# The overflow rows spread in two passes, batches 0 to 3 first and 4 to 7 added, and a new written order

## The chip, the cores and the metric

The kernel runs on one core of a Trainium2 chip. The metric is the device time of one execution, in microseconds (us). TensorE does the matmuls (PE in the profile), VectorE (DVE) and ScalarE (ACT) do the elementwise work and empty the matmul results out of PSUM, GpSimd (POOL) issues nearly all transfers, and the sync engine (SP) issues the first few.

## The reference

Linear attention and, on its result, a layer of eight experts with hash routing. Attention, for 8 batches of 8 heads, 576 tokens and head width 64, then the experts over all 4608 tokens of width 512:

```python
q_s = softmax(q, axis=-1); k_s = softmax(k, axis=2)
kv  = np.einsum('bhsd,bhse->bhde', k_s, v)
x   = np.einsum('bhsd,bhde->bhse', q_s, kv)      # then tokens x 512
expert_idx = token_ids * 2654435761 % 8
for e in range(8):
    mask = expert_idx == e
    h = np.maximum(x[mask] @ w1[e], 0.0)         # 512 -> 1024
    out[mask] = h @ w2[e]                        # 1024 -> 512
```

## The kernel before

Every expert has 640 slots for tokens: 72 for each of the 8 batches (576, five blocks of rows with the last half full) and 64 more for its overflow, the tokens that did not fit into the 72 of their batch. An index stage of about 11 us computes from the token ids which row of q goes into which slot. Then the rows of q are gathered slot by slot with indirect transfers, softened, transposed, and multiplied by their batch's `kv`, so that the expert's input stands in slot order, transposed, in `XT`. The overflow tokens of all experts are gathered apart, by batch pair, multiplied by `kv` (`xov0` to `xov3`, one for two batches each), and then spread to the experts' overflow slots (`XTov`) with one-hot matrices `Qs`.

The work is cut into named steps. A list written out by hand, `ORDER`, says in which order they are issued; each engine carries out its own in that order, and so does GpSimd with its transfers. A set `SWAP` says which of the copies that may go to either of ScalarE and VectorE leave their usual engine. The steps, with e an expert, b a batch, i a block or a part:

- `K b`, `V b`, `G e_i`, `GO_i`, `W e1_i`, `W e2_i`: transfers, on GpSimd's queue (K0 to K2 on the sync engine's): k and v of a batch, gathers of q rows for an expert's block or the overflow, and the halves of an expert's two weight matrices. L781, L785, L395, L508.
- `EK b`, `MK b`, `EQ e_i`: on ScalarE, the exponentials of k (two instructions, L354 and L355), the column of ones beside v, the exponential of a gathered block (L406).
- `KV b`: on TensorE, 20 matmuls to k-transposed times v (L372); `SC b`: on VectorE, four instructions that divide by the sums into `kvrs` (L381 to L387).
- `SM e`, `ML e` (with a or b for the blocks): on VectorE, the row sums of the exponentials and their reciprocals (L418 to L420), and the scaling (L424). `TP e_i`, `TC e_i`: transposes on TensorE (L436), copy out of PSUM (L879, L875 for the overflow `TCO`).
- `PP e_lo r`, `PC e_lo r`: matmuls of transposed q with `kvrs` (L447, L459), batches from lo, quarter r of the width; copy into `XT` (L907, L913).
- `XP n`, `XC n`: the same for the overflow of batches 2n and 2n+1 (L469, L886). `SH r`, `SD r`: the spreading of quarter r, four matmuls that add up over n (L476), and its copy into `XTov` (L482).
- `FND`, `FDD`, `QS`, `ROP`, `ROD`: the overflow's index work.
- `A e_lo_i`, `R e_lo_i`: the first expert product from slot lo on (L523) and its relu. `A0_576_0` is the one that reads `XTov` for expert 0; for the others `OV e` copies `XTov` into `XT`. `B e_blk`, `C e_blk`, `S e_blk`: the second product of a block (L545), its copy out (L936, L938) and its scatter into the output (L550).

`NAME*n` in the list puts n warming matmuls ahead of that step's own (L345). PSUM has eight banks in three kinds, and a step of TensorE waits until a bank of its kind has been emptied: two of T (XP, SH, B and others), two of Q (TP and PP of the first four experts), two double ones of S (KV, A, later PP). The second buffer of the weights holds the exponentials of k until the last KV is done, so the second expert's weights wait for that. Odd batches' k has one buffer, even batches' two; a load waits for the exponential that reads its buffer, and v waits for the KV of the batch whose buffer it takes.

Of the kernel before, what the change touches and what calls it, by code (L numbers as in the profile page):

```python
# [701 lines left out]
W31_0 EQ5_3 PP2_32 G5_0 PP2_01 PC2_01 G6_0 EQ5_2 R1_320_0 B1_1 EQ4_0 PC2_32 PP2_33 R1_320_3 PP2_30 PC2_33
EQ5_4 PC2_30 W31_1 G5_1 B1_0 C1_1 C1_0 PP2_02 SM4a PP2_03 B1_2 PC2_02 PP2_31 PC2_03 OV5 OV4 PP2_00 EQ4_3 B1_3
C1_2 W22_0 G7_0 PC2_31 PC2_00 A2_0_0 PP2_63 W22_1 G7_4 ML4a PP2_60 G6_3 A2_0_1 PC2_63 PP2_61 R2_0_0 EQ5_0
R2_0_1 PC2_61 PC2_60 S0_1 B1_4 OV2 A2_320_1 R2_320_1 EQ5_1 SM5b A3_0_1 W32_1 R3_0_1 S0_3 G7_3 A2_0_2 G6_4
TP4_0 S1_1 S0_0 R2_0_2 A2_320_3 R2_320_3 A2_320_2 ML5b A2_0_3 SM5a ML5a W32_0 C1_4 R2_320_2 A3_320_2 R2_0_3
A3_0_0 R3_320_2 G6_1 R3_0_0 A2_320_0 A3_0_3 TP5_3 TC4_0 TC5_3 R2_320_0 TP4_2 B2_3 R3_0_3 C1_3 A3_0_2 A3_320_0
EQ4_4 W41_0 R3_0_2 R3_320_0 TP5_0 TC5_0 A3_320_3 A3_320_1 C2_3 W41_1 B2_1 SM4b ML4b TP5_2 R3_320_3 R3_320_1
C2_1 EQ7_1 B2_4 EQ6_1 PP4_01 TC4_2 PP4_00 TC5_2 G7_2 EQ7_0 C2_4 TP4_3 EQ7_3 PC4_01 B3_1 PC4_00 S1_2 W51_1 S2_4
TC4_3 C3_1 PP4_30 EQ6_0 EQ6_2 S1_0 B2_0 PP4_60 EQ6_4 PC4_30 OV6 PC4_60 PP4_31 B2_2 SM6a C2_0 PP4_61 W51_0 ML6a  # L710
PC4_31 C2_2 EQ7_2 PC4_61 OV7 EQ7_4 A4_0_1 SM7b S1_4 B3_4 C3_4 R4_0_1 TP6_2 A4_320_0 B3_3 R4_320_0 W42_0
A4_320_2 R4_320_2 S3_4 SM7a EQ6_3 A4_0_3 TP6_0 TC6_2 R4_0_3 S2_1 W42_1 A4_320_1 TC6_0 R4_320_1 A4_320_3
R4_320_3 B3_2 ML7b ML7a A5_320_2 A5_320_1 R5_320_2 C3_2 A4_0_2 TP7_3 S2_2 S3_1 R4_0_2 R5_320_1 TP7_0 B3_0
A5_0_0 TC7_0 C3_3 R5_0_0 SM6b TP7_2 A4_0_0 W52_1 TC7_2 R4_0_0 A5_0_2 C3_0 S1_3 B4_1 R5_0_2 A5_320_3 R5_320_3
PP6_00 B4_0 A5_0_1 PC6_00 ML6b A5_320_0 C4_1 C4_0 TP6_3 R5_0_1 PP6_01 B4_3 TC7_3 W52_0 S3_0 R5_320_0 B4_4 C4_4
# [295 lines left out]
```

## Time and profile before

| | us |
|---|---|
| Median of 3 runs | 224.19 (224.01 to 224.94) |
| Profiled execution | 224.46 |
| Its span, first to last instruction | 222.6 |
| TensorE busy in it | 189.1 (85%) |
| VectorE, ScalarE, GpSimd busy | 137.8, 116.6, 122.9 |

The span is what the trace shows; the time of the execution is longer by what lies around it. In timelines a row is one or more like instructions of one engine, with the idle time ahead of it and what ended it in brackets; lengths of successive rows of TensorE overlap a little, since matmuls are pipelined, so costs are best taken from one start to the next. The granted clock is the share of TensorE's full clock.

### The profile page before, as it was taken

The page shows a single profiled execution, that of the slowest core. Times are in us where ns is not written, and L with a number is a line of the kernel's source. Part 1 is how long each engine was busy: PE and PEld are TensorE (multiplying, and loading weights), DVE is VectorE, ACT ScalarE, POOL GpSimd, SP SyncE. Part 2 cuts the span into 40 slices and gives each one's busy share as a digit, 9 for nine tenths or more (in the row PEclk, how much of TensorE's full clock was granted, in tenths as well). Part 3 has the DMA queues.
Part 4 walks back from the last instruction along what each step waited for, and adds up shares of the span by engine and source line. Part 5 has one row for each costly group of instructions (what it writes and reads, how often), then busy time and mean ns, then how long its engine had stood idle before and what let it go on. Part 6 is the DMA issues. An engine that isn't in the chain of part 4 may idle for free.

```text
span 222.6 us, 3981 instructions
## 1 busy us (share of the span) xinstructions
PE 189.1 (85%) x1533; PEld 124.1 (56%) x1533; DVE 137.8 (62%) x259; ACT 116.6 (52%) x189; POOL 122.9 (55%) x160
## 2 busy tenths in 40 slices
...
GB/s 209 321 329 389 234 345 329 322 245 296 292 280 274 292 247 267 221 244 233 266 308 216 239 146 155 148 165 3 175 234 167 188 186 195 284 110 135 166 165 85
DMA packets 13543, 50.67 MB, mean 228 GB/s; under 512 B 2650, under 2 KB 2650, under 8 KB 12496
## 3 DMA queue, kind: packets, MB, share of 16 engines
...
q1 hardware_dynamic: 576, 3.71, 4.3%
...
## 4 chain that ended last, share of the span: by engine, by line
issue 38%; POOL 21%; PE 20%; DMA 11%; DVE 6%; ACT 2%; POOLq 1%; DVEq 0%
POOL out_dram L550 12%; PE ph L523 7%; DMA kraw<-in_k_dram 4%; PE po L545 4%; DMA out_dram<-ob,sidx 3%; DMA w1r<-in_moe_w_dram 3%; POOL raw L395 3%; PE t L372 2%; POOL w1r L508 2%; PE t L436 2%; PE t L476 2%; POOL w2r L508 2%; DVE A L126 1%; PE t L447 1%; PE t L469 1%
## 5 line engine op out<-in xcount | busy, mean ns | idle before, releaser
L545 PE MATMUL po<-w2r,hT 128*128 128x512 f16 (+2 forms) x328 | 74.8, 374 | 0.0
L523 PE MATMUL ph<-XT,w1r 128*128 128x320 f16 (+2 forms) x512 | 74.6, 297 | 0.0
L536 ACT ACTIVATE hT<-ph 128x640 f16<-128x640 f32 (+3 forms) x58 | 40.5, 703 | 55.3 <-PE ph L523 54.6
L550 POOL DMA_INDIRECT out_dram<-ob,sidx x40 | 42.6, 1065 | 44.7 <-DVE ob L938 29.6
L523 PEld LDWEIGHTS <-w1r 128*128 128x128 f16 x544 | 49.3, 98 | 21.2
L395 POOL DMA_INDIRECT raw<-in_q_dram,gidx x40 | 42.9, 1071 | 20.7 <-issue 4.9
L938 DVE TENSOR_SCALAR ob<-po 128x512 f32<-128x512 f32 x34 | 23.1, 683 | 43.8 <-PE po L545 39.4
L545 PEld LDWEIGHTS <-hT 128*128 128x128 f16 x328 | 30.9, 98 | 30.4
L418 DVE TENSOR_REDUCE rq<-qs 128x16 f32<-128x1024 f16 (+1 forms) x18 | 26.1, 1450 | 3.8 <-ACT qs L406 3.7
L424 DVE TENSOR_TENSOR qs<-qs,rq 128x1024 f16<-128x1024 f16 (+1 forms) x18 | 26.1, 1456 | 0.4
L406 ACT ACTIVATE qs<-raw 128x512 f16<-128x512 f32 (+1 forms) x40 | 23.6, 625 | 0.8 <-DMA raw<-in_q_dram,gidx 0.8
L436 PE MATMUL t<-ident,qs 128*128 128x128 f16 (+1 forms) x176 | 15.8, 226 | 4.8 <-ACT qT L879 2.6
L879 DVE COPY qT<-t 128x512 f16<-128x512 f16 (+3 forms) x18 | 8.5, 478 | 15.6 <-PE t L436 15.3
L508 POOL DMA_DIRECT2D w2r<-in_moe_w_dram x16 | 9.5, 595 | 14.3 <-PE po L545 10.1
L436 PEld LDWEIGHTS <-qs 128*128 128x128 f16 (+1 forms) x176 | 12.0, 103 | 9.1 <-issue 4.3
L372 PE MATMUL t<-v,w1r 128*128 128x129 f16 x64 | 8.0, 293 | 7.5 <-ACT v L360 7.5
L508 POOL DMA_DIRECT2D w1r<-in_moe_w_dram x16 | 9.5, 595 | 5.8 <-PE ph L523 3.7
L372 PEld LDWEIGHTS <-w1r 128*128 128x128 f16 x64 | 6.9, 139 | 7.5 <-issue 7.4
L372 PE MATMUL t<-v,w2r 128*128 128x129 f16 x64 | 5.9, 243 | 5.9 <-DVE rec L381 5.9
L907 DVE CAST XT<-t 128x288 f16<-128x288 f32 (+2 forms) x18 | 7.9, 453 | 4.2 <-PE t L447 3.9
L913 ACT CAST XT<-px 128x864 f16<-128x864 f32 (+1 forms) x7 | 5.6, 811 | 8.6 <-PE px L459 8.6
L879 ACT COPY qT<-t 128x512 f16<-128x512 f16 (+2 forms) x14 | 7.9, 581 | 3.9 <-PE t L436 3.9
...
## 6 DMA issues: line engine op xcount, KB each, us to landing
...
```

The lines of the kernel that those rows point to most:

```text
L372: nc.tensor.matmul(pkv[:, r // 2, r % 2, 0:129], lhsT=k16t[:, f] if last else k16[:, c, f], rhs=v16s[e][:, c * NPAIR + r, 0:129] if last e ...
L395: nc.gpsimd.indirect_dma_start(out=raw[0:w, :], out_offset=None, in_=self.q[:, :], in_offset=bass.IndirectOffsetOnAxis(ap=idx[0:w, i:i + 1 ...
L406: self.nc.scalar.activation(q16[0:w, i].rearrange("p h d -> p (h d)"), raws[i][0:w, :], ACT.Exp)
L418: nc.vector.reduce_sum(rv, qv, axis=AX.X)
L424: nc.vector.tensor_tensor(out=qf, in0=qf, in1=rv.rearrange("p i h -> p (i h)").unsqueeze(2) .to_broadcast([w, (hi - lo) * H_, DH_]), op=AL ...
L436: nc.tensor.transpose(pv[:, r, o:o + w[j]], q16[0:w[j], j, 2 * r:2 * r + 2, :] .rearrange("p h d -> p (h d)"), self.ident[0:w[j], 0:w[j]])
L508: self.nc.gpsimd.dma_start(w[what - 1][:, 2048 * i:2048 * i + 2048], src[e, :, 2048 * i:2048 * i + 2048])
L523: nc.tensor.matmul(p, lhsT=w1r[:, dc, f[i] * 128:(f[i] + 1) * 128], rhs=X[:, dc, :], start=(dc == 0), stop=(dc == DC - 1))
L536: self.nc.scalar.activation(to, fro, ACT.Relu)
L545: nc.tensor.matmul(po[:, 0:d.stop - d.start], lhsT=hT[:, fc, blk * 128:(blk + 1) * 128], rhs=w2r[:, fc, d], start=(fc == 0), stop=(fc == F ...
L550: sc = self.nc.gpsimd.indirect_dma_start(out=self.out[:, :], out_offset=bass.IndirectOffsetOnAxis(ap=self.ix.sidx[:, e, blk:blk + 1], axis=0),
L938: nc.vector.tensor_scalar(out=obs[e, blk][:, d], in0=po[e, blk, x][:, 0:d.stop - d.start], scalar1=1.0 / SX, scalar2=None, op0=ALU.mult)
```

## The change

`shared` takes the batch pairs that it adds up. `SH r` now spreads pairs 0 and 1 (batches 0 to 3), `SD r` copies that into `XTov`; a new step `SI r` spreads pairs 2 and 3, and a new step `SE r` adds its result to what stands in `XTov`, on VectorE. All of `ORDER` and `SWAP` is written anew. In the new list the steps ahead of the first expert product and a few behind it, and the last ones, are these (the middle is left out; it holds the same steps as before in another order):

```diff
@@ -470,16 +470,21 @@
                                  rhs=self.kvrs[2 * n + j][:, r, :], start=(j == 0), stop=(j == 1))
         return pt
 
-    def shared(self, xovs, Qs, r):
+    def shared(self, xovs, Qs, r, ns):
         pr = self.bank("T")
-        for n in range(NBP):
+        for n in ns:
             self.nc.tensor.matmul(pr[:], lhsT=xovs[n][:, r * 128:(r + 1) * 128], rhs=Qs[n],
-                                  start=(n == 0), stop=(n == NBP - 1))
+                                  start=(n == ns[0]), stop=(n == ns[-1]))
         return pr
 
     def spread(self, pr, r):
         put = self.nc.scalar.copy if other(f"SD{r}", r % 2 == 1) else self.nc.vector.tensor_copy
         put(self.XTov[:, :, r, :], pr[:].rearrange("p (e i) -> p e i", e=E_MOE))
+
+    def join(self, pr, r):
+
+        x = self.XTov[:, :, r, :]
+        self.nc.vector.tensor_tensor(out=x, in0=pr[:].rearrange("p (e i) -> p e i", e=E_MOE), in1=x, op=ALU.add)
 
 
 def other(name, put):
@@ -678,48 +683,48 @@
 
 SWAP = set("""
-TC0_4 PC0_00 PC0_43 R0_0_3 TCO_3 R0_0_2 R0_0_1 PC0_62 PC0_60 PC0_63 SD2 SD1 TC1_1 SD0 PC1_40 C0_1 PC1_00
-PC1_01 C0_2 TC2_3 C0_0 PC1_43 TC3_3 TC2_2 TC2_1 TC3_0 R1_0_1 PC2_32 R1_320_3 C1_1 C1_0 PC4_01 PC4_00 PC4_31
-TC6_3 C7_4a C7_4b
+TCO_1 PC1_03 SD0 PC0_01 TCO_2 PC0_42 PC1_01 PC0_41 XC2 PC0_62 R0_0_2 PC0_61 R0_432_1 C0_4 TC3_3 TC3_4 TC2_0
+PC2_60 R1_0_2 R1_0_0 PC2_01 PC2_30 PC2_03 PC2_33 C0_3 R2_320_1 C1_1 R3_320_2 R3_320_0 C2_2 PC4_31 C2_1 C2_0
+PC6_01 C6_4 R7_0_1 C7_4a C7_4b
 """.split())
 
 ORDER = """
-MK0 EK1 MK1 CNT G0_2 EK0 G0_0 EQ0_2 OVA ZO1 KV1 G0_1 EQ0_0 KV0 EQ0_1 ZO0 OHA FND K3 FDD G0_3 V2 EK2 QS SM0a
-EQ0_3 G0_4 MK2 EQ0_4 EK3 V3 SC0 GO_1 SC1 KV2 ML0a SM0b K4 TP0_0 G1_4 MK3 TP0_1 KV3 GO_0 EQO_0 V5 ML0b K5 EQO_1
-GO_3 TC0_0 TC0_1 SMOa TP0_3 MLOa TC0_3 SC3 TP0_4 GO_2 TC0_4 SC2 ROP V4 MK5 TP0_2 TC0_2 TPO_1 K6 EK5 EQO_3 V6
-ROD TPO_0 TCO_0 TCO_1 MK4 XP1 EQO_2 PP0_03*4 SMOb EK4 MLOb EK6 G1_3 KV5 W01_0 SC5 PP0_00 MK6 PC0_00 EQ1_4 KV4
-SC4 PC0_03 PP0_40*4 EQ1_3 W01_1 PP0_41 XP0 XC1 PC0_41 PP0_43 K7 PC0_43 PC0_40 TPO_2 PP0_01 SM1b TCO_2 PC0_01
-V7 KV6 PP0_02 PP0_42 PC0_42 PC0_02 XP2 G1_2 XC0 TPO_3 EK7 MK7 ML1b A0_0_3 G3_4 SC6 G1_0 A0_0_2 R0_0_3 TCO_3
-TP1_4 G2_1 G1_1 R0_0_2 EQ1_2 TC1_4 A0_0_1 W02_1 TP1_3 KV7 R0_0_1 TC1_3 A0_0_0 SC7 XP3 PP0_62 PP0_60 XC2 G2_4
-EQ1_0 PC0_62 G3_3 PC0_60 PP0_63 EQ1_1 PP0_61 G2_3 XC3 PC0_63 SH3 SM1a SH2 PC0_61 W02_0 SD3 SD2 SH1 SH0 G2_2
-ML1a A0_432_0 TP1_2 G2_0 TP1_1 EQ3_4 SD1 W11_1 G3_1 EQ2_3 TC1_1 SD0 A0_576_0 R0_0_0 EQ2_4 TC1_2 SM2b G4_2 G4_1
-W11_0 G3_2 G3_0 OV1 EQ3_3 TP1_0 B0_1 TC1_0 R0_576_0 W12_1 OV3 R0_432_0 PP1_40 G5_3 PC1_40 PP1_41 PC1_41 C0_1
-A0_432_1 PP1_42 EQ2_0 EQ2_1 ML2b R0_432_1 PP1_00 PC1_00 PC1_42 B0_2 TP2_3 PP1_01 B0_0 G4_4 EQ2_2 PC1_01 C0_2
-W21_1 SM3b ML3b PP1_03 G5_2 TC2_3 PP1_43 C0_0 PC1_03 SM2a B0_3 PC1_43 PP1_02 TP3_3 EQ3_0 PC1_02 TC3_3 G4_3
...
-S6_0 C6_1 S7_0 S5_1 B7_1 R7_320_2 A7_320_3 C7_1 S4_2 B6_3 S7_1 C6_3 S6_1 S6_3 R7_320_3 B7_2 C7_2 B7_3 S7_2
-C7_3 B7_4a C7_4a B7_4b S7_3 C7_4b S7_4
+G0_2 G0_1 CNT OVA EK0 OHA FND FDD EK1 QS G0_0 EQ0_1 EK2 K3 ROP G1_1 EQ1_1 G1_2 MK1 V3 G1_0 EQ0_2 MK0 ZO0 ZO1
+EQ0_0 SM0a KV0 MK3 EQ1_2 V2 GO_1 EQ1_0 ML0a G0_4 TP0_1 EK3 SC0 TP0_0*3 K4 MK2 KV1 GO_2 TC0_1 TP0_2 EQO_1 SM1a
+GO_0 TC0_0 EQ0_4 ML1a TC0_2 SC1 KV3 EK4 TP1_0 EQO_0 TP1_2 G0_3 KV2 SMOa MLOa SC2 TC1_2 TP1_1 TC1_1 TPO_1*3 K5
+G1_3 SC3 GO_3 EQ1_3 TC1_0 TCO_1 TPO_0*4 V4 G1_4 EQ0_3 PP0_00 V5 ROD SM0b XP1 EK5 ML0b K6 TCO_0 PP1_03 PC0_00
+PP0_02 XP0 MK4 V6 K7 V7 EQO_2 KV4 W01_0 SC4 PC1_03 PC0_02 W01_1 PP1_02 G3_2 EQ1_4 XC1 PC1_02 XC0 G3_0 PP0_03
+SH0 G2_4 MK5 TP0_3 SH1 SD0 SM1b PC0_03 SH3 PP0_01 TC0_3 EQO_3 KV5 EK6 G3_1 G3_3 SMOb MK6 W11_0 TP0_4 MLOb
+PC0_01 G2_3 PP1_00 SD1 KV6 TC0_4 ML1b SC5 G2_2 TPO_2*4 PC1_00 SD3 SH2 TCO_2 PP0_42 EK7 MK7 PP0_43 PC0_43
+PC0_42 TP1_3 TP1_4 G3_4 KV7 W11_1 TC1_4 SC6 TPO_3 SD2 TC1_3 TCO_3 PP1_01 XP2 W02_1 PP0_40 SC7 G4_3 PC1_01
+PP0_41 XP3 PC0_40 PP0_62 PC0_41 XC2 PP1_41 W02_0 PC0_62 PP1_40 XC3 PC1_41 SI1 PP0_63 SI0 PC1_40 PC0_63 G2_0
+SE1 EQ3_2 PP1_43 G2_1 PC1_43 PP0_60 A0_0_2 SE0 A0_0_1 R0_0_2 EQ3_0 EQ3_1 PP0_61 PC0_61 SI2 A0_0_3 R0_0_1 G5_3
+PC0_60 SI3 R0_0_3 EQ2_4 SM3a EQ2_3 A0_0_0 A0_432_0 PP1_42 SE3 SE2 W12_1 A0_576_0 ML3a G5_0 G5_2 R0_0_0 PC1_42
+SM2b TP3_0 R0_432_0 EQ3_3 OV1 A0_432_1 TP3_1 R0_432_1 A1_0_1 TC3_0 A1_320_0 G5_1 ML2b EQ2_2 G4_0 TP3_2 EQ3_4
+R1_0_1 W12_0 TC3_2 A1_320_2 R1_320_0 G6_3 TP2_4 R1_320_2 TC3_1 R0_576_0 A1_0_3 SM3b EQ2_0 A1_320_1 B0_4 ML3b
+R1_320_1 EQ2_1 TC2_4 G4_1 TP2_3 G5_4 TC2_3 SM2a W21_0 B0_1 C0_4 TP3_3 R1_0_3 TC3_3 A1_0_2 ML2a TP3_4 B0_0
...
+S4_0 A7_320_0 C6_0 S4_3 B7_0 B6_1 C7_0 R7_320_0 A7_320_1 B7_1 R7_320_3 C6_1 R7_320_1 S6_0 B7_3 C7_1 C7_3 B7_2
+C7_2 S7_0 B7_4a S6_1 B7_4b S6_2 S7_1 S7_3 C7_4a S7_2 C7_4b S7_4
 """.split()
@@ -887,8 +892,10 @@
                 add(f"XP{n}", lambda n: po.update({("x", n): at.overflow(n, qTo)}), n)
                 add(f"XC{n}", xovc, n)
             for i in range(NPAIR):
-                add(f"SH{i}", lambda i: pr.update({i: at.shared(xovs, Qs, i)}), i)
+                add(f"SH{i}", lambda i: pr.update({i: at.shared(xovs, Qs, i, (0, 1))}), i)
                 add(f"SD{i}", lambda i: at.spread(pr[i], i), i)
+                add(f"SI{i}", lambda i: pr.update({i: at.shared(xovs, Qs, i, (2, 3))}), i)
+                add(f"SE{i}", lambda i: at.join(pr[i], i), i)
 
             for e in range(1, E_MOE):
                 add(f"OV{e}", lambda e: V(xt(e // 2)[:, e % 2, :, MAINC:CAP], at.XTov[:, e]), e)
```

## Rows read from the trace of the kernel before

**Rows 1.** The page: its first line, one execution.

```profile
span 222.6 us, 3981 instructions
```

**Rows 2.** Windows: stretch, its length, busy us (instructions) of each engine, granted clock, DMA share, GB/s.

```profile
core 0: us, PE busy (x) PEld busy (x) DVE busy (x) ACT busy (x) POOL busy (x), PEclk, DMA share, GB/s
35.00:40.00 5.00, 2.73 (x48) 2.28 (x48) 3.62 (x7) 3.67 (x8) 2.57 (x5) 0.61 1.05 338
45.00:50.00 5.00, 5.00 (x43) 3.96 (x42) 3.17 (x8) 4.50 (x6) 2.14 (x2) 0.53 1.05 242
...
56.24:216.70 160.46, 160.06 (x1195) 99.40 (x1192) 92.82 (x145) 80.44 (x135) 87.96 (x96) 1.00 0.85 207
```

**Rows 3.** Timeline of TensorE: start, length in us, engine, line, operation.

```profile
56.24 3.08 PE L523 MATMUL ph<-XT,w1r 128*128 128x432 f16 x16
61.17 0.39 PE L372 MATMUL t<-v,w2r 128*128 128x129 f16 x4
62.31 1.62 PE L523 MATMUL ph<-XT,w1r 128*128 128x432 f16 x8
...
65.12 3.62 PE L476 MATMUL t<-Q,xov 128*128 128x512 f16 x16
...
69.57 0.61 PE L436 MATMUL t<-ident,qs 128*128 128x128 f16 x8
70.02 1.10 PE L523 MATMUL ph<-XTov,w1r 128*128 128x64 f16 x32
...
72.90 0.42 PE L447 MATMUL t<-qT,kvr 128*128 128x72 f16 x8
73.16 1.17 PE L523 MATMUL ph<-XT,w1r 128*128 128x144 f16 x16
...
210.62 6.01 PE L545 MATMUL po<-w2r,hT 128*128 128x512 f16 x35
```

**Rows 4.** Three DMA issues of GpSimd, each with its time to landing under it.

```profile
39.92 0.53 POOL L508 DMA_DIRECT2D w1r<-in_moe_w_dram  x1 [1.95 <-DMA rawo<-in_q_dram,oidx]
DMA to landing us min/median/max: 14.9/14.9/14.9
...
43.38 1.05 POOL L395 DMA_INDIRECT raw<-in_q_dram,gidx  x1 [0.47 <-DMA v<-in_v_dram]
DMA to landing us min/median/max: 17.4/17.4/17.4
...
52.62 1.00 POOL L395 DMA_INDIRECT raw<-in_q_dram,gidx  x1 [0.52 <-DMA w1r<-in_moe_w_dram]
DMA to landing us min/median/max: 10.5/10.5/10.5
```

**Rows 5.** Timeline of ScalarE, idle time before in brackets.

```profile
34.92 1.15 ACT L406 ACTIVATE qs<-rawo 128x512 f16<-128x512 f32 x2 [3.92 <-DMA rawo<-in_q_dram,oidx]
...
39.66 1.91 ACT L354 ACTIVATE w1r<-kraw 128x2048 f16<-128x2048 f32 x1
...
42.23 0.63 ACT L406 ACTIVATE qs<-rawo 128x512 f16<-128x512 f32 x1
```

**Rows 6.** Timeline of VectorE.

```profile
36.10 1.22 DVE L418 TENSOR_REDUCE rq<-qs 128x16 f32<-128x1024 f16 x1 [1.31 <-ACT qs L406]
...
37.92 1.23 DVE L424 TENSOR_TENSOR qs<-qs,rq 128x1024 f16<-128x1024 f16 x1
...
39.18 0.16 DVE L381 TENSOR_SCALAR rec<-t 128x4 f32<-128x4 f32 x1
...
40.48 0.29 DVE L879 COPY qT<-t 128x256 f16<-128x256 f16 x1
...
62.51 0.16 DVE L381 TENSOR_SCALAR rec<-t 128x4 f32<-128x4 f32 x1 [0.30 <-PE t L372]
```

**Rows 7.** Groups of the page: busy us, mean ns of one, idle before.

```profile
L938 DVE TENSOR_SCALAR ob<-po 128x512 f32<-128x512 f32 x34 | 23.1, 683 | 43.8 <-PE po L545 39.4
L907 DVE CAST XT<-t 128x288 f16<-128x288 f32 (+2 forms) x18 | 7.9, 453 | 4.2 <-PE t L447 3.9
```

More of the change, by code (lines that the diff above doesn't have):

```diff
@@ L697 @@
-A0_432_1 PP1_42 EQ2_0 EQ2_1 ML2b R0_432_1 PP1_00 PC1_00 PC1_42 B0_2 TP2_3 PP1_01 B0_0 G4_4 EQ2_2 PC1_01 C0_2
-W21_1 SM3b ML3b PP1_03 G5_2 TC2_3 PP1_43 C0_0 PC1_03 SM2a B0_3 PC1_43 PP1_02 TP3_3 EQ3_0 PC1_02 TC3_3 G4_3
-A1_320_1 A1_0_3 ML2a R1_320_1 TP2_4 EQ3_2 A1_0_2 TP3_4 TC2_4 R1_0_3 W12_0 TP2_2 TC3_4 EQ3_1 S0_2 W21_0
-A1_320_2 R1_0_2 TC2_2 A1_0_0 SM3a PP2_62 EQ4_2 TP2_1 PC2_62 B0_4 TC2_1 G4_0 R1_0_0 C0_3 TP2_0 A1_0_1 ML3a
-TP3_2 G5_4 R1_320_2 TC2_0 A1_320_3 C0_4 TP3_0 TC3_2 TP3_1 TC3_0 R1_0_1 EQ4_1 S0_4 A1_320_0 G7_1 G6_2 TC3_1
@@ L702 @@
[L702 to L715, printed above, removed]
-C4_3 A5_0_3 W61_1 S4_0 TC6_3 PC6_01 W61_0 B5_4 PP6_31 C5_4 B4_2 PC6_31 PP6_30 B5_3 S3_3 R5_0_3 S4_4 PC6_30
@@ L717 @@
-W71_0 A6_0_1 C4_2 PP6_60 S3_2 C5_3 B5_2 PC6_60 PP6_61 R6_0_1 A6_0_2 C5_2 B5_1 W62_1 S5_3 W62_0 R6_0_2 A6_0_3
-PC6_61 R6_0_3 B5_0 S5_2 A6_320_0 W71_1 S4_1 R6_320_0 S2_3 A6_320_2 R6_320_2 A6_320_3 C5_1 R6_320_3 A6_0_0
-A6_320_1 R6_0_0 B6_0 C5_0 S5_4 A7_0_2 W72_0 S2_0 R6_320_1 R7_0_2 S5_0 A7_0_0 B6_4 R7_0_0 A7_320_1 W72_1 C6_4
-S4_3 A7_0_1 C6_0 B6_2 R7_320_1 S6_4 A7_0_3 R7_0_1 R7_0_3 C6_2 A7_320_0 S6_2 B7_0 B6_1 A7_320_2 R7_320_0 C7_0
-S6_0 C6_1 S7_0 S5_1 B7_1 R7_320_2 A7_320_3 C7_1 S4_2 B6_3 S7_1 C6_3 S6_1 S6_3 R7_320_3 B7_2 C7_2 B7_3 S7_2
```

20 lines of the change are left out of this document (added).

## Prediction

> **What bounds the kernel now.** I read the forty slices and the windows first, then TensorE's timeline, then the landings of the loads, then ScalarE and VectorE ahead of the first expert product. The profiled execution took 224.46 us, its span is 222.6 us [rows 1], so 1.9 us lie around it; the median of the runs shown, 224.19, is 0.27 below that execution. Three things are to be seen. First, from A0_0_3 at 56.24 TensorE never rests: 160.06 busy of 160.46, clock 1.00 [rows 2], up to the last matmul at 210.62 + 6.01 = 216.63 [rows 3]. Second, before that it waits for loads: the transfer engines are full (1.05) in every stretch shown [rows 2], so a load lands when all that was queued before it has, not when it is issued: W01_1 took 14.9 us to land [rows 4]. Third, TensorE idles so much there that its clock is 0.61 and 0.53 of full in two of these stretches [rows 2], mostly the 1.2 GHz level. So the time is: when the first expert product starts, plus the TensorE work left from there, plus a tail of 222.6 - 216.63 = 6.0 us. The new order leaves the last scatters (S7_3, S7_2, S7_4 behind B7_4) in the same relation to the last matmul, so I keep the tail.
>
> **TensorE work that crosses the first expert product.** In the new order A0_0_2 is the first, and ahead of it stand steps that before came after. KV7: 61.17 to 62.31, 1.14 us. Five TP1: eight transposes from 69.57 to 70.02 are two of them, 0.45, so 1.1. XP3 is also eight matmuls of 128 columns, 0.45. Ten PP0 and PP1: two take 72.90 to 73.16, so 1.3. Twelve of the sixteen matmuls of the spreading, which took 3.62: 2.7 [all rows 3]. With the 0.4 of idle time [rows 2] that is 7.1 us. Left from the first expert product: 216.63 - 56.24 - 7.1 = 153.3 us. **Break-even:** the new A0_0_2 must start at 216.63 - 153.3 = 63.3. The spreading's count of matmuls stays sixteen; the extra warming matmuls (14 against 8) all lie ahead of A0 in time that waits anyway.
>
> **When the weights are there.** W01_0 and W01_1 move behind K7 and V7 and behind G1_0, G1_1, G1_2. What GpSimd has queued up to W01_1 in the new order is exactly what it had up to G1_2 before, plus G1_0 and G1_1. G1_2 landed at 43.38 + 17.4 = 60.8, and G1_1, four gathers later, at 52.62 + 10.5 = 63.1 [rows 4], so a gather costs 0.6. The weights land at 60.8 + 1.2 = 62.0; before at 39.92 + 14.9 = 54.8. No order of the compute engines makes A0 earlier than that.
>
> **When the engines are ready.** VectorE is the longest queue ahead of A0. SMOa waits for EQO_0, which stands behind EK4 on ScalarE. Before, the overflow gathers had landed when EQO_0 started, at 34.92 [rows 5]; in the new order three G1 gathers are ahead of them and two others are not, so +0.6. EK4 with its second exponential and EQO_0 take 42.23 + 0.63 - 39.66 = 3.2 [rows 5]; started near 35 they end at 38.0 (37.6 to 38.4). From there VectorE has, up to SC7: four pairs of sums and scaling (SMOa, SM0b, SM1b, SMOb, and MLOa, ML0b, MLOb, ML1b), a pair 36.10 to 39.18 less small gaps, 3.0, together 12.0; SC2 to SC6 at 39.18 to 40.48, 1.30 each, 6.5 [rows 6]; TCO_1, TCO_2, PC0_03, PC0_43, PC0_42, at most 0.45 each [rows 7], 2.1; ROD, four of some 0.16 like the small one at 39.18 [rows 6], 0.7; SD2, near the 0.68 of L938 [rows 7], 0.7. Sum 22.0, SC7 starts at 60.0. Before, from the start of SC7 (62.51 [rows 6]) through XP3 and XC3 to the first spreading matmul (65.12 [rows 3]) it took 2.6. Then SI1 and SI0 (0.45 each) and three PP (0.4 with a bank wait): 1.2. So A0_0_2 could start at 60.0 + 2.6 + 1.2 = 63.8 if nothing on that queue waits.
>
> One thing may: SC4 needs KV4. VectorE reaches SC4 10.0 us of that queue after 38.0, at 48.0. TensorE can begin XP1, PP1_03, PP0_02, XP0, KV4 after TCO_1, at 44.1, and needs 2.3 us at full clock and 4.6 at half, with hand-overs to ScalarE up to 5. So SC4 is late by 0 to 1.0. Before, the stretch 45 to 50 ran at 0.53 [rows 2]; I take 0.6. **A0_0_2 at 64.4**, that is 1.1 after break-even.
>
> **The joins.** SE0 to SE3 are new, each an addition over 512 columns with one operand in PSUM. No such addition is in the trace; the nearest row, the 128x512 result copy out of PSUM, takes 0.68 [rows 7], below it nothing is likely, above it I allow 0.8. Together 2.7 to 3.2 us on VectorE, less two copies that go to ScalarE. They are hidden: SE1 and SE0 run under A0_0_2, SE3 and SE2 under A0_0_0, and their first reader, A0_576_0, comes some 8 us after A0_0_2. Without that cover TensorE would wait 0.7 for each.
>
> **Behind the first product** the supply is thinner. W02_0 is behind W01_1 by four fetches and nine gathers. A fetch of 512 KB at 207 to 242 GB/s [rows 2] is 2.2 to 2.5 us; 62.0 + 9.6 + 5.4 = 77.0. B0_4, its first user, has some 16 us of TensorE work between A0_0_2 and itself, so 80.5: 3.5 to spare. I add 0.3 of small waits in the long stretch. **Sum: +1.1 + 0.3 = +1.4**, 225.9 for the profiled execution, 225.6 against the median.
>
> **Rivals.** (1) VectorE's queue is shorter than I count, and the weights are last: SC7 starts by 58.3, A0 at 62.1. Then -1.2 + 0.3 = -0.9, 223.3, the only way below before. For it: the spreading's first pass is out of the end, and my sum has no wait in it to remove. Against: it needs 1.7 us less than 22.0.
> (2) TensorE's clock falls again. Between KV6 (about 53) and KV7 (about 58) it has only TPO_2 with its warming matmuls, SH2, two PP and two TP1, some 2.5 us; before, a similar lull left 35 to 40 at 0.61 [rows 2]. Then KV7, XP3, SI and the PP, some 3 us, double, of which about 2 is on the path, and 2 to 4 us of expert products run at half, 1 to 2 more: +2.5 to +5, 227.6. It decides from the point at which the fall reaches KV7. The Trainium skill, "TensorE: Matmul & The Clock Gate", section "The HAM clock gate", says that the throttled state is the default and activity releases it; the 0.61 agrees, and by that rule alone the time would be this rival's.
> (3) The weights run dry behind A0: if the queue slips by 5 us, B0_4 waits 1.5: +2.9, 227.1. For it: every transfer there is back to back. Against: the 3.5 us.
> (4) The split itself does nothing: the first pass still waits for its own copies and only the order acts. The time is then the forecast's.
>
> **How the numbers follow.** Forecast, with (4): 0.58, its own range +0.2 to +2.3 (A0 from 63.3 to 65.3, and the small waits). (1) 0.15, (2) 0.20, (3) 0.07. Within 0.5%, 1.1 us, which is about what a measurement of this kernel can tell: 0.26 of the forecast and most of (1), 0.11, together 0.37. Faster: the rest of (1), 0.04, since its bound is -0.9 to -1.2. Slower: 0.59. Range: up to the middle of (2), 227.9, down into (1), 223.7.
>
> **What would show it.** A0_0_2 starting between 63.3 and 65.3, with VectorE busy without a gap from 38 to SC7 and SC7 the last to release XP3; W01_1 landing at 62; 153 us of unbroken TensorE from there. Wrong if A0 starts with the landing, if the granted clock is below 1.00 after 58, or if TensorE has more than 1 us of idle time behind A0.

## The result and the profile after

The changed kernel takes 225.72 us (median of 13 executions, 224.57 to 227.32), the kernel before 224.59 beside it (13 executions, 223.63 to 225.25): ratio 1.0061, 95% interval 1.0036 to 1.0086. It is slower by 1.1 us; the forecast was 225.6. On another chip the same two kernels later took the same time (the last row of the table below). The medians here and below are of all executions, while the ratios leave out slow ones: in the table two of the run placed anew and one each of the runs with both edits and with KV4 early.

The traced execution is the fastest of those 13, at 224.57 us, and it alone, beside 224.46 for the traced execution before, would say "no change". The first page lines, its span and the granted clock in 40 slices:

```profile
span 222.3 us, 3991 instructions
...
PEclk9999999999999999999999999999999999999998
```

Windows, with the columns of [rows 2]; the third begins at the first expert product, A0_0_2, and ends with the last matmul:

```profile
35.00:40.00 5.00, 2.94 (x39) 2.21 (x37) 3.28 (x9) 4.37 (x6) 2.68 (x4) 1.00 1.05 358
45.00:50.00 5.00, 3.98 (x56) 2.92 (x56) 4.75 (x9) 4.42 (x12) 3.59 (x4) 1.00 1.03 322
63.30:216.56 153.26, 153.26 (x1104) 94.43 (x1100) 85.05 (x128) 69.59 (x114) 82.58 (x92) 1.00 0.84 203
```

TensorE's granted clock is 1.00, its 2.4 GHz level, in both stretches where it was 0.61 and 0.53 in [rows 2], and behind A0_0_2 TensorE has 153.26 us of work without a rest. So in this execution the new order does two things that cancel: it makes the first expert product begin 7.06 us later (63.30, before 56.24), and leaves 7.13 us less behind it (216.56 against 216.63 at the end).

TensorE's timeline: the first and the last row of KV4, then the start of KV7, XP3, SI1, SI0, A0_0_2, A0_576_0 (which reads the joined `XTov`), and B0_4, the first second product:

```profile
45.48 0.39 PE L372 MATMUL t<-v,w1r 128*128 128x129 f16 x4
...
46.56 0.22 PE L372 MATMUL t<-v,kt 128*128 128x129 f16 x1
...
58.32 0.40 PE L372 MATMUL t<-v,w2r 128*128 128x129 f16 x4
...
60.89 0.70 PE L469 MATMUL t<-kvr,qTo 128*128 128x128 f16 x8
...
62.18 0.59 PE L476 MATMUL t<-Q,xov 128*128 128x512 f16 x2
...
62.67 0.60 PE L476 MATMUL t<-Q,xov 128*128 128x512 f16 x2
...
63.30 1.44 PE L528 MATMUL ph<-XT,w1r 128*128 128x432 f16 x7
...
71.20 1.10 PE L528 MATMUL ph<-XTov,w1r 128*128 128x64 f16 x32
...
79.56 0.81 PE L550 MATMUL po<-w2r,hT 128*128 128x512 f16 x3
```

VectorE's: SMOa, SC4, SC7, and the joins SE1, SE0, SE3 with SE2:

```profile
38.07 1.22 DVE L418 TENSOR_REDUCE rq<-qs 128x16 f32<-128x1024 f16 x1 [1.50 <-ACT qs L406]
...
47.88 0.16 DVE L381 TENSOR_SCALAR rec<-t 128x4 f32<-128x4 f32 x1
...
59.73 0.15 DVE L381 TENSOR_SCALAR rec<-t 128x4 f32<-128x4 f32 x1
...
63.21 0.69 DVE L487 TENSOR_TENSOR XTov<-t,XTov 128x512 f16<-128x512 f32 x1
...
64.19 0.68 DVE L487 TENSOR_TENSOR XTov<-t,XTov 128x512 f16<-128x512 f32 x1
...
68.81 1.29 DVE L487 TENSOR_TENSOR XTov<-t,XTov 128x512 f16<-128x512 f32 x2 [0.42 <-PE t L476]
```

No bracket stands at SC4: KV4 was there in time. TensorE began XP1 and the steps up to KV4 at 44.13, where the forecast had them (44.1), and was done at 46.78, 1.1 ahead of SC4: 2.65 us at a granted clock of 1.00, for which the forecast had 2.3, and 4.6 at half clock. From 38.07 to SC7 the timeline shows one gap on this queue, 0.32 us. The issue of W01_0 and W01_1, the second at 44.91, and below it the two times to landing (the longer is W01_1's, so 62.3):

```profile
L513 POOL DMA_DIRECT2D w1r<-in_moe_w_dram x2: 563/568/572, 44.4 to 44.9; - x2
...
DMA to landing us min/median/max: 15.4/16.4/17.4
```

### The profile page after: what moved, and what is told of

Its sections match the earlier page's. It is cut to its first block, busy times and chain, and to the rows that moved or that the text cites. A ratio compares the mean times of both kernels' runs of the same rounds, so it can differ in the third digit from the quotient of the medians.

```text
span 222.3 us, 3991 instructions
## 1 busy us (share of the span) xinstructions
PE 187.6 (84%) x1539; PEld 121.5 (55%) x1539; DVE 138.9 (62%) x260; ACT 117.2 (53%) x192; POOL 123.6 (56%) x160
## 4 chain that ended last, share of the span: by engine, by line
PE 58%; DMA 12%; DVE 11%; issue 9%; POOL 6%; ACT 1%; POOLq 0%; SPq 0%; DVEq 0%
PE ph L528 28%; PE po L550 23%; DMA kraw<-in_k_dram 9%; POOL out_dram L555 5%; DMA raw<-in_q_dram,gidx 3%; PE t L436 3%; DVE kvr L387 2%; DVE qs L424 2%; DVE rq L418 2%; PE px L459 2%; PE t L447 1%; PE t L476 1%; DVE XT L914 1%; POOL raw L395 1%; POOL v L790 1%
## 5 line engine op out<-in xcount | busy, mean ns | idle before, releaser
L555 POOL DMA_INDIRECT out_dram<-ob,sidx x40 | 41.4, 1036 | 53.3 <-DVE ob L945 42.8
L541 ACT ACTIVATE hT<-ph 128x640 f16<-128x640 f32 (+3 forms) x55 | 38.2, 710 | 56.8 <-PE ph L528 55.7
L528 PEld LDWEIGHTS <-w1r 128*128 128x128 f16 x544 | 49.1, 98 | 21.0
L395 POOL DMA_INDIRECT raw<-in_q_dram,gidx x40 | 45.2, 1131 | 22.2 <-issue 5.5
L945 DVE TENSOR_SCALAR ob<-po 128x512 f32<-128x512 f32 x32 | 21.9, 685 | 44.7 <-PE po L550 44.7
L447 PE MATMUL t<-qT,kvr 128*128 128x72 f16 (+1 forms) x96 | 8.2, 206 | 4.2 <-DVE qTo L880 1.8
L943 ACT ACTIVATE ob<-po 128x512 f32<-128x512 f32 (+2 forms) x9 | 4.9, 552 | 12.1 <-PE po L550 12.1
L543 DVE TENSOR_SCALAR hT<-ph 128x640 f16<-128x640 f32 (+2 forms) x8 | 6.7, 842 | 6.4 <-PE ph L528 6.2
L447 PEld LDWEIGHTS <-kvr 128*128 128x128 f16 x96 | 6.3, 98 | 7.4 <-issue 4.3
L884 ACT COPY qT<-t 128x512 f16<-128x512 f16 (+1 forms) x13 | 6.8, 534 | 6.4 <-PE t L436 6.4
```

The source lines that it names most:

```text
L395: nc.gpsimd.indirect_dma_start(out=raw[0:w, :], out_offset=None, in_=self.q[:, :], in_offset=bass.IndirectOffsetOnAxis(ap=idx[0:w, i:i + 1 ...
L447: nc.tensor.matmul(pv[:, :, i * CELL:(i + 1) * CELL], lhsT=self.kvrs[b][:, r, :], rhs=qT[:, r, q0 + es.start:q0 + es.stop, b * CELL:(b + 1 ...
L528: nc.tensor.matmul(p, lhsT=w1r[:, dc, f[i] * 128:(f[i] + 1) * 128], rhs=X[:, dc, :], start=(dc == 0), stop=(dc == DC - 1))
L541: self.nc.scalar.activation(to, fro, ACT.Relu)
L555: sc = self.nc.gpsimd.indirect_dma_start(out=self.out[:, :], out_offset=bass.IndirectOffsetOnAxis(ap=self.ix.sidx[:, e, blk:blk + 1], axis=0),
L945: nc.vector.tensor_scalar(out=obs[e, blk][:, d], in0=po[e, blk, x][:, 0:d.stop - d.start], scalar1=1.0 / SX, scalar2=None, op0=ALU.mult)
```

## The experiments

**The theory**: the time is the start of A0_0_2 plus 153.26 us and the tail, and that start is set by VectorE's queue from SMOa to SC7; break-even is a start at 63.3. The rivals: TensorE's clock; weights that run dry behind A0_0_2; and that the split does nothing and only the order acts. All runs are in this table, with the chip on which they ran (numbered 1 to 4 in the order of the runs) and that chip's median of the kernel before. The changed kernel itself ran on chips 1 and 4 and not on 2 and 3, so a version on chip 2 or 3 is compared with it across chips. "Left" is from A0_0_2 to the last matmul, in the traced execution.

| run | chip | median us (executions) | before | ratio (95%) | A0_0_2 | left |
|---|---|---|---|---|---|---|
| changed, unaltered again | 1 | 225.89 (8) | 224.82 | 1.0059 (1.0033 to 1.0086) | 63.53 | 153.26 |
| no split | 1 | 228.35 (5) | 224.82 | 1.0185 (1.0151 to 1.0218) | 64.57 | 154.12 |
| more warming | 1 | 226.6 (6) | 224.82 | 1.0098 (1.0065 to 1.0131) | 63.58 | 153.26 |
| no warming | 1 | 226.68 (7) | 224.82 | 1.0076 (1.0047 to 1.0105) | 64.26 | 153.79 |
| weights early | 2 | 226.17 (12) | 224.57 | 1.0049 (1.0023 to 1.0076) | 63.94 | 154.29 |
| W31_0 late | 2 | 226.12 (12) | 224.57 | 1.0071 (1.0048 to 1.0093) | 64.63 | 154.81 |
| EQO_0 early | 2 | 224.90 (12) | 224.57 | 1.0028 (1.0002 to 1.0054) | 63.14 | 153.26 |
| both | 2 | 225.76 (12) | 224.57 | 1.0044 (1.0017 to 1.0071) | 64.14 | 153.25 |
| placed anew | 3 | 230.32 (6) | 226.35 | 1.0118 (1.0068 to 1.0168) | 68.22 | 153.27 |
| split in the old order | 3 | 232.41 (6) | 226.35 | 1.0282 (1.025 to 1.0314) | | |
| KV4 early | 4 | 229.1 (6) | 226.19 | 1.0101 (1.0061 to 1.0142) | 67.07 | 154.79 |
| changed, a third time | 4 | 226.25 (12) | 226.19 | 1.0000 (0.9972 to 1.0027) | 63.71 | 154.21 |

**The changed kernel unaltered, again.** No edit.

> The changed kernel once more, unaltered. Its profiled execution took 224.57 us, 0.1 over the one of the kernel before, but the median of its executions is 225.72. Theory: in the profiled execution TensorE kept its full clock from 34 us on, and in most others it falls once or twice in the gaps between 38 and 62 us, which costs 0.5 to 3 us on the way to the first expert product or in it. Then this profile, if it is one of the longer executions, has a granted clock below 1.00 somewhere between 38 and 70, A0_0_2 starts later than 63.3 by about the difference, and the median is again 225.3 to 226.2. Rival: the loads come later or the stretch behind A0 has idle time in the longer executions; then the clock is as in the first profile and the weights land after 62.5, or TensorE has idle time after 64.

The ratio came out the same, and the trace again had a stretch of 153.26 us without a rest behind A0_0_2. With no wait in it, the "left" of an order is a constant, and only the start moves. The clock was below 1.00 here in one place, 0.66 in 40 to 45 us, and A0_0_2 is 0.23 later than in the first trace.

**No split.** SH and SD of the first pass are gone, and one pass over all four pairs stands where SI and SE stood. What were the joins are plain copies, all of them on VectorE (the edit to `SWAP` isn't shown):

```diff
-add(f"SH{i}", lambda i: pr.update({i: at.shared(xovs, Qs, i, (0, 1))}), i)
+add(f"SH{i}", lambda i: pr.update({i: at.shared(xovs, Qs, i, (0, 1, 2, 3))}), i)
...
-add(f"SI{i}", lambda i: pr.update({i: at.shared(xovs, Qs, i, (2, 3))}), i)
-add(f"SE{i}", lambda i: at.join(pr[i], i), i)
```

> The new order with the spreading in one pass: the first pass and its copies are gone, all four matmuls of a quarter stand where the second pass stood, and what were the joins are plain copies on VectorE. Theory: eight matmuls of 512 columns, 1.7 us, leave idle time ahead of the first expert product and come into the unbroken stretch or right before it; VectorE's queue ahead of SC7 loses one copy of 0.7, but SC7 still needs KV7, so it gains 0.2 to 0.5. The kernel is slower than the changed one by 1.0 to 1.6 us. Rival: the first pass only fills time that waits and its copies hold up VectorE and ScalarE as much as it saves; then within 0.4.

The spreading of two quarters now stands whole ahead of A0_0_2 (TensorE's timeline of this run):

```profile
62.59 1.03 PE L476 MATMUL t<-Q,xov 128*128 128x512 f16 x4
63.45 0.23 PE L447 MATMUL t<-qT,kvr 128*128 128x72 f16 x2
63.51 1.03 PE L476 MATMUL t<-Q,xov 128*128 128x512 f16 x4
...
64.57 1.63 PE L528 MATMUL ph<-XT,w1r 128*128 128x432 f16 x8
```

A0_0_2 starts 1.04 later than in the unaltered run, and 0.86 more is left behind it: 1.9 of the 2.0 us between the two spans (225.0 and 223.0). Four matmuls account for 0.86 of it on either side (above, SI1 with its two is 0.49 ahead of SI0, a short PP between). The other 0.18 of the later start was there before the first spreading matmul (62.59, against 62.41 in the unaltered run). So the split is worth about 2 us here by the traces, 2.5 by the two medians, more than I expected: it moves eight matmuls into time in which TensorE waits. That only the order acts is refuted.

**More warming, no warming.** The first adds 19 warming matmuls, the second takes all 14 away:

```diff
-XP1
+XP1*6
...
-SH0
+SH0*3
...
-KV6
+KV6*5
...
-TPO_2*4
+TPO_2*9
```

```diff
-TP0_0*3
+TP0_0
...
-TPO_1*3
+TPO_1
...
-TPO_0*4
+TPO_0
...
-TPO_2*4
+TPO_2
```

> The new order with 19 more warming matmuls in TensorE's gaps: six ahead of XP1, which now stands ahead of PP0_00, three ahead of SH0, five ahead of KV6, which now stands ahead of PP1_00, and nine instead of four ahead of TPO_2. Theory: the long executions are those in which the clock falls, so the median comes down to 224.6 to 225.0, the spread from 2.7 to about 1 us, and the clock is 1.00 from 45 on in every execution. Rival: the spread is of the loads or of something else; then the median stays at 225.4 to 226 with the same spread.

> The new order without its 14 warming matmuls. Theory: TensorE's gaps grow, the clock falls in more executions and later, and the median rises by 0.7 to 2.5 us over the changed kernel; the profile has a stretch at half clock between 45 and 65. Rival: the warming matmuls do nothing here; within 0.4 of the changed kernel.

More warming didn't lower the median. But it didn't make the clock fuller either (the means over an execution are 0.985 to 0.997, unaltered on the same chip 0.987 to 0.997), so the run doesn't tell what a fuller clock would be worth. Without warming the forecast's case happens: the clock is 0.65 in 40 to 45 us and 0.67 in 45 to 50, KV4 takes 46.74 to 48.80, and SC4 waits (VectorE's timeline of the run without warming):

```profile
48.84 0.16 DVE L381 TENSOR_SCALAR rec<-t 128x4 f32<-128x4 f32 x1 [0.76 <-PE t L372]
```

A0_0_2 then starts at 64.26, near where the forecast put it (64.4). In the traces of the unaltered kernel, with its warming matmuls, that wait is absent.

**Weights early; W31_0 late.** W11_1, W02, W21_1, W31, W22_1 and W42 issued a few steps sooner; and, alone, W31_0 one gather later:

```diff
-G2_3 PP1_00
+G2_3 W11_1 PP1_00
...
-W21_0 B0_1
+W21_0 W21_1 B0_1
...
-A2_320_1 G6_4
+A2_320_1 W31_1 W31_0 G6_4
```

```diff
-W31_0 A2_320_2 R2_0_0 G7_1 W22_0
+A2_320_2 R2_0_0 G7_1 W31_0 W22_0
```

> The new order with weight fetches moved ahead on GpSimd's queue, nothing else: W11_1 ahead of G2_2 and G3_4, W02_1 and W02_0 ahead of G4_3, W21_1 right behind W21_0, both W31 ahead of G6_4, S0_1 and G6_2, W22_1 right behind W22_0, both W42 ahead of S3_4 and S0_2. In the first profile of the changed kernel six weight halves land only 0.3 to 1.2 us ahead of their first matmul (W31_0 0.29, W21_1 0.45, W42_0 0.62, W11_1 0.73, W01_1 0.97, W02_0 1.20), and with no warming matmuls A3_320_1 is seen to wait for its weights. Theory: in the longer executions transfers are a little slower and TensorE waits at these places; that is the 1 us between the profiled execution and the median. Then the median falls by 0.6 to 1.2 us below that of the changed kernel, to 224.7 to 225.3, and the profiled execution stays near 224.6. Rival: the difference lies ahead of A0_0_2; then the median stays within 0.3.

> The new order with W31_0 behind G7_1 instead of ahead of it: one gather later on GpSimd's queue, 1.3 us of its issue time and 0.65 of transfer. Theory of the thin supply: W31_0, which had 0.3 us to spare, lands 0.7 to 1.4 later, A3_320_1 waits 0.4 to 1.1 in the profile, and the median rises by about as much. Rival, supply with room: no wait, no change.

In the unaltered kernel's trace W31_0 lands 0.29 us ahead of its first user; one gather more, and TensorE waits (waits of TensorE behind A0_0_2, W31_0 late):

```profile
PE ph L528 <- DMA w1r<-in_moe_w_dram: 1.4, 1, 1.4
```

So the supply is thin at W31_0. But with the weights earlier no gain is seen: 1.0049 is within the unaltered kernel's interval from chip 1, and so is the 1.0071 of W31_0 late. With the weights early the gather G4_4, now behind W21_1, landed later in the traced execution; its exponential (ScalarE) then held the copy that TensorE needed:

```profile
98.39 0.63 ACT L406 ACTIVATE qs<-raw 64x512 f16<-64x512 f32 x1 [2.30 <-DMA raw<-in_q_dram,gidx]
98.93 0.50 ACT L914 CAST XT<-t 128x432 f16<-128x432 f32 x1
```

```profile
99.47 0.35 PE L447 MATMUL t<-qT,kvr 128*128 128x144 f16 x3 [0.88 <-ACT XT L914]
```

The run with both edits has the same fetches and no such wait (153.25 left).

**EQO_0 early, and both.** EQO_0 ahead of EK4 on ScalarE; then this with the early weights:

```diff
-KV3 EK4 TP1_0 EQO_0 TP1_2
+KV3 EQO_0 EK4 TP1_0 TP1_2
```

> The new order with EQO_0 ahead of EK4 on ScalarE, nothing else. Theory of the prediction: VectorE's queue from SMOa to SC7 sets the first expert product. SMOa then starts at 36.6 to 36.8 instead of 38.1, and SC7 as soon as KV7 is done, 59.0 to 59.2 instead of 59.7 to 60.0; A0_0_2 starts at 62.5 to 62.8 instead of 63.3 to 63.5, now close on the landing of W01_1 (62.3), and the profiled execution is 0.5 to 0.9 us shorter than those of the changed kernel. The median falls less, by 0 to 0.7, since the weights behind A0 then land with still less to spare. Rival: the landing of the weights sets A0_0_2; then it stays at 63.3 to 63.5 although SC7 is earlier.

> Both edits: the weight fetches ahead, and EQO_0 ahead of EK4. Theory: the earlier first expert product is kept only if the weights behind it come earlier too, so the median falls by 1.0 to 1.8 us below the changed kernel, to 224.1 to 224.9, equal to the kernel before or below it by up to 0.7. Rival: no better than the better of the two.

SMOa starts 1.13 earlier than at 38.07 and the queue moves up, until SC4 finds KV4 unfinished and gives 0.89 back (VectorE's timeline, EQO_0 early):

```profile
36.94 1.22 DVE L418 TENSOR_REDUCE rq<-qs 128x16 f32<-128x1024 f16 x1 [0.35 <-ACT qs L406]
...
47.61 0.16 DVE L381 TENSOR_SCALAR rec<-t 128x4 f32<-128x4 f32 x1 [0.89 <-PE t L372]
```

The ratio is the lowest of the altered versions, 1.0028, 0.7 us below the unaltered kernel's 1.0059. That gain is not shown: the unaltered kernel never ran on this chip, its own ratio differs by 0.006 between chips 1 and 4, and A0_0_2 starts 0.16 earlier than in its first trace, 0.39 and 0.57 earlier than in the others. On one chip, this edit stands alone only between the runs weights early and both: 226.17 and 225.76, ratios 1.0049 and 1.0044. In the trace of both, KV4 fell into a stretch at a granted clock of 0.50, the 1.2 GHz level (46.15 to 48.53), SC4 waited 1.85, and A0_0_2 came at 64.14.

**Placed anew; split in the old order.** The first puts EQO_0, EK5, EQO_3, SD2 and KV7 where the theory wanted them, and the weights but W21_1 early; since EQO_3 then writes the buffer from which TP0_3 has yet to read, expert 0's fourth block is transposed from overflow rows and its own result isn't computed, with all instructions the same in number and size; only the times of this run count. The second takes the order of the kernel before with the split alone.

```diff
-SM0b XP1 EK5 ML0b
+SM0b XP1 ML0b
...
-XP0 MK4 V6 K7 V7 EQO_2 KV4
+XP0 MK4 EK5 V6 K7 V7 EQO_2 EQO_3 KV4
...
-EK7 MK7 PP0_43 PC0_43 PC0_42 TP1_3 TP1_4 G3_4 KV7
+EK7 MK7 KV7 SD2 PP0_43 PC0_43 PC0_42 TP1_3 TP1_4 G3_4
```

```diff
-A0_0_3 G3_4 SC6 G1_0 A0_0_2
+A0_0_3 G3_4 SC6 G1_0 SH0 SD0 SH1 SD1 A0_0_2
...
-R0_0_2 EQ1_2 TC1_4 A0_0_1
+R0_0_2 EQ1_2 TC1_4 SH2 SD2 SH3 SD3 A0_0_1
...
-SH3 SM1a SH2 PC0_61 W02_0 SD3 SD2 SH1 SH0
+SI3 SM1a SI2 PC0_61 W02_0 SE3 SE2 SI1 SI0
```

> The new order with the split kept, and its steps placed anew: EQO_0 ahead of EK4 as in the run with EQO_0 early, EK5 behind MK4, EQO_3 behind EQO_2, SD2 on ScalarE, KV7 right behind MK7, and the weight halves W11_1, W02, W31, W22_1 and W42 each a few gathers earlier on GpSimd. Theory of the VectorE queue (the start of A0 is set by VectorE's steps from SMOa to SC7): SC7 starts at about 59.1 us, A0 at about 62.5, right at W01_1's landing (62.3), and with 153.26 us of TensorE left the profiled execution takes 223.6 to 224.2 us and the median is 224.0 to 224.8, level with the kernel before or up to 0.6 below it. Rival, that what the new order costs is not in that queue but in the executions' spread behind A0 (clock, weights): A0 comes earlier in the profile, but the median stays at 225.5 or more.

> The order of the kernel before with the split of the spread alone: SH0 to SH3 as the first pass, from batches 0 to 3, at places between the matmuls ahead of A0_0_1 and A0_0_2, and batches 4 to 7 added where SH and SD stood. Theory that the split is worth something only where TensorE stands idle waiting (in the new order in front of A0): the old order has TensorE unbroken there, the same columns are multiplied, so the time is within 0.4 us of the kernel before, or up to 0.4 above it for the four joins on VectorE. Rival, that the split gains by itself (shorter accumulations): 1 us or more below the kernel before. Rival, that the joins cost by themselves: 1 us or more above.

Both missed widely. Placed anew, A0_0_2 starts at 68.2 instead of 62.5. ScalarE's timeline shows why: EK5, which in the unaltered kernel ran at 41.16, ahead of them, now stands ahead of EQO_2, XC1 and XC0, and all of it down to EK7 (58.13; 55.21 in the run with EQO_0 early) is late:

```profile
45.19 1.92 ACT L354 ACTIVATE w1r<-kraw 128x2048 f16<-128x2048 f32 x1
...
47.79 1.15 ACT L406 ACTIVATE qs<-rawo 128x512 f16<-128x512 f32 x2
...
50.70 0.59 ACT L891 CAST xov<-t 128x512 f16<-128x512 f32 x1
...
58.13 1.93 ACT L354 ACTIVATE w2r<-kraw 128x2048 f16<-128x2048 f32 x1
```

KV7 ahead of PP0_43 did its part: TensorE stood 1.75 us for MK7, and the copy behind it waited (VectorE's timeline):

```profile
62.41 0.52 DVE L914 CAST XT<-t 128x144 f16<-128x144 f32 x2 [3.18 <-PE t L447]
```

In the old order the split costs 6.1 us by the medians. TensorE has no idle time there to move matmuls into, and the waits agree with each pass holding one of two T banks until VectorE or ScalarE has emptied it (waits of TensorE from 57 us, 6.6 in sum; the 1.5 has no releaser in the trace):

```profile
PE t L476 <- DVE XTov L487: 2.2, 1, 2.2
PE t L476 <- DVE XTov L482: 1.8, 2, 1.0
PE t L447 <- issue: 1.5, 1, 1.5
PE ph L528 <- DVE XTov L487: 1.1, 1, 1.1
```

The traced execution is the slowest of the six (234.70), its first product starts at 57.52 (before 56.24), and behind it the granted clock was 0.93 in 70 to 75 us and 0.73 in 75 to 80; so the waits don't add up to the 6.1. The rest of that run's order was not made for joins, so 6.1 is the price of this placement, not of the additions, 0.7 each.

**KV4 early; a third trace.** EQO_0 early, and KV4, MK4 and EK5 ahead of PP0_00, TPO_2 ahead of KV6; and once more the unaltered kernel, for an execution nearer its median.

```diff
-KV3 EK4 TP1_0 EQO_0 TP1_2
+KV3 EQO_0 EK4 TP1_0 TP1_2
...
-EQ0_3 PP0_00 V5 ROD SM0b XP1 EK5 ML0b
+EQ0_3 EK5 MK4 KV4 PP0_00 V5 ROD SM0b XP1 ML0b
...
-G2_3 PP1_00 SD1 KV6 TC0_4 ML1b SC5 G2_2 TPO_2*4
+G2_3 TPO_2*4 PP1_00 SD1 KV6 TC0_4 ML1b SC5 G2_2
```

> The order of the run with EQO_0 early, and the wait of SC4 taken away: EK5 and MK4 stand ahead of TCO_0, KV4 ahead of PP0_00 and XP1 on TensorE (so it starts at about 45.0 us rather than 46.3), and TPO_2 with its warming matmuls ahead of PP1_00 and KV6, so that TCO_2 doesn't hold VectorE in its turn. Theory of several limits: VectorE has 0.9 us less ahead of it, but SC7 also needs KV7, and that needs the last load of k and v; in the run with EQO_0 early K7 landed at 54.79, V7 at 57.30, EK7 ended at 57.79 and KV7 ran 58.15 to 59.46, so SC7 can't start before about 59.2, A0 not before 62.7, and VectorE idles instead. Median within 0.4 us of the run with EQO_0 early, 0 to 0.5 above the kernel before, not below it. Rival, that VectorE's queue alone sets the start: SC7 at 58.7 or earlier, A0 at 62.2, and a median 0.5 us or more below the kernel before.

> The changed kernel unaltered, traced a third time. Its two traced executions (224.57 and 225.12 us) were the lowest of 13 and of 8, so they don't show where the usual one, at 225.7 to 225.9, spends its last microsecond. If that lies ahead of A0 (VectorE's queue, clock), an execution near the median shows A0 at 63.9 to 64.5 and again 153.3 us of TensorE behind it; if it lies behind, A0 is at 63.3 to 63.6 and TensorE waits for weights or copies for 0.7 us or more.

With KV4 early SC4 didn't wait, and VectorE stood still later, 2.45 us for EQO_3, because KV4, for which TensorE stood 1.98 us waiting on MK4, had pushed XP1 and XP0 back (XP1 46.24, before 44.26), and with them XC0, SH0, SD0 and EQO_3 on ScalarE (52.54, before 49.64). VectorE's timeline (SC4, SMOb, SC7), then ScalarE's (EQO_3, EK6, EK7):

```profile
46.96 0.16 DVE L381 TENSOR_SCALAR rec<-t 128x4 f32<-128x4 f32 x1
...
53.22 1.22 DVE L418 TENSOR_REDUCE rq<-qs 128x16 f32<-128x1024 f16 x1 [2.45 <-ACT qs L406]
...
62.33 0.16 DVE L381 TENSOR_SCALAR rec<-t 128x4 f32<-128x4 f32 x1 [0.59 <-PE t L372]
```

```profile
52.54 0.64 ACT L406 ACTIVATE qs<-rawo 128x512 f16<-128x512 f32 x1
53.07 1.91 ACT L354 ACTIVATE w2r<-kraw 128x2048 f16<-128x2048 f32 x1
...
58.13 1.92 ACT L354 ACTIVATE w2r<-kraw 128x2048 f16<-128x2048 f32 x1
```

The theory of one queue falls with this. SC7 (59.73 in the unaltered order) has three queues that end close ahead of it: VectorE's own; TensorE's, where KV7 ran from 58.32 to 59.63, behind two transposes that had waited for a VectorE copy; and ScalarE's to EK7 and MK7, which was done at 57.64, some 0.7 ahead of KV7. Here KV7 waited 0.69 for EK7 instead. Of the theory of several limits the direction held, its size did not: I named K7's and V7's landing as what would hold A0_0_2 at 62.7, and overlooked ScalarE's queue, which put SC7 at 62.33. Behind SC7 another 1.2 was lost (4.74 to A0_0_2, 3.57 in the unaltered kernel), where TensorE waited 1.31 for a copy of VectorE; the granted clock was 0.66 in 50 to 55 us.

The third trace is of an execution of 226.28 us, at its median of 226.25. EK4 stands behind the copy of a transpose, which comes late: TP0_2 took 34.34 to 34.98, its four matmuls 0.63, in the first trace 0.39. So SMOa is at 38.48 (ScalarE: TC0_2, EK4, EQO_0):

```profile
35.01 0.59 ACT L884 COPY qT<-t 128x512 f16<-128x512 f16 x1 [1.33 <-PE t L436]
35.50 1.91 ACT L354 ACTIVATE w1r<-kraw 128x2048 f16<-128x2048 f32 x1
...
37.83 0.62 ACT L406 ACTIVATE qs<-rawo 128x512 f16<-128x512 f32 x1
```

A0_0_2 starts 0.41 later than in the first trace (63.71), and behind it A0_576_0's last two matmuls come late:

```profile
73.26 0.23 PE L528 MATMUL ph<-XTov,w1r 128*128 128x64 f16 x2 [0.46 <-issue]
```

That puts what follows 0.78 back, a smaller delay before B1_1 0.18; with the start that is 1.4 of the 1.9 by which the span is longer (224.2 against 222.3). The other 0.5 lies behind the last matmul: 6.3 us to the end of the span, 5.7 in the first trace, 6.2 in the second. "Issue" says that nothing in the trace explains the pause. So part lies ahead of A0_0_2 and part behind it, and neither of the two outcomes expected came whole. On this chip the kernel before takes as long (226.19), so the trace doesn't say where the 1.1 us on chip 1 lies.

## Why the prediction was right, and where it was not

**Work that crosses the first product: right.** 153.3 us was forecast to be left; 153.25 to 153.27 was measured in every trace with the split in the new order and no wait behind A0_0_2.

**The split, rival (4): wrong as a rival.** The forecast had counted the twelve spreading matmuls that come ahead of A0_0_2 (2.7 us) among those that cross; that count is where the split acts, and the run without it shows what it is worth, some 2 us. The joins were hidden as forecast, 0.69, 0.68 and 1.29 for two, done 1.1 us ahead of A0_576_0.

**The weights: right.** W01_1 landed at 62.33 (forecast 62.0), W02_0 at 78.4 (77.0), with 1.2 to spare against 3.5. They did not run dry in the unaltered kernel's three traces, but W31_0 had 0.29 in hand, and in the traces without warming and with W31_0 late TensorE waited 0.4 and 1.4 for it. Rival (3) didn't happen; the place nearest to it was another weight than the one it named.

**VectorE's queue: right in size, incomplete as a limit.** SMOa 38.07 (38.0), SC7 59.73 (60.0), and from there 3.57 to A0_0_2 (3.8). What was missed is that TensorE's queue to the end of KV7 is done only 0.1 ahead of SC7, and ScalarE's to MK7 only some 0.7 ahead of KV7; in the orders placed anew and with KV4 early KV7 waited for ScalarE.

**The term that was mis-sized is KV4's wait.** It was put at 0.6, from the old kernel's clock in 45 to 50 us, and A0_0_2 at 64.4, 1.1 behind break-even. TensorE had its full clock there, KV4 was done 1.1 ahead, and SC4 didn't wait in any trace of the unaltered kernel, and A0_0_2 came at 63.30, 63.53 and 63.71, 0 to 0.4 behind break-even; in the two runs that move only weights behind W01_1 it came at 63.94 and 64.63.

**Where the 1.1 us is instead.** On the chip of the first four runs the median span is 223.0 for the kernel before and 223.75 unaltered, 0.75 more; what lies around the span is 1.83 and 2.14, 0.31 more. The forecast kept that constant (1.9) and the tail (6.0, measured 5.7, 6.2 and 6.3). The 0.31 is in every execution. What makes up the 0.75 is not shown: the one trace near the median is from chip 4, and there it is a later start (0.4), pauses behind it (1.0) and a longer tail. So the direction and the reasons given for it, the work left, the landing and VectorE's queue, held, but that the total came out to 0.1 us is luck: the start was put 0.7 to 1.1 too late, 0.3 outside the span wasn't in the sum, and pauses and tail came out below the forecast in one trace and above it in another.

**The clock, rival (2): mostly wrong.** Between KV6 and KV7 the clock fell in none of the unaltered traces (1.00 from 45 us up to the tail; 0.66 in 40 to 45 in one). The Trainium skill, "TensorE: Matmul & The Clock Gate", section "The HAM clock gate", has TensorE throttled by default and released by activity; by it alone 227.6 was worked out in the forecast, and the traces of the unaltered kernel, with a granted clock of 1.00 at that point, don't bear that time out. The clock fell there in the traced execution with W31_0 late, whose edit lies far behind that point: KV7 took 58.62 to 60.39, and A0_0_2 came at 64.63. The slices of that execution, the eleventh from 56.5 us:

```profile
PEclk9999999999799999999999999999999999999997
```

Over the 21 executions of the unaltered kernel on the first two occasions, the 11 with a mean clock of 0.992 or more have a median of 225.54, the other 10 of 226.1. So the clock goes with a part of the spread; that it causes it isn't shown, and the upper group too is above the kernel before.
